# The experts' first product as seven quarter products, with operands streamed from DRAM

## The chip, the cores and the metric

One Trainium2 chip, and on it one core. The metric is the device time of one execution in microseconds (us). A core has TensorE (PE in the profile, with its weight loads as PEld), VectorE (DVE), ScalarE (ACT), GpSimd (POOL) and SyncE (SP), each with its own queue of instructions; the DMAs of this kernel are issued from SP.

## What is computed

Three stages follow one another: attention with feature maps, a first MLP, and a layer of 8 experts, all of which see all 2304 tokens. The experts' weights are 8 x 512 x 1024 and 8 x 1024 x 512:

```
x = attention(q, k, v, w_phi)                 # 4 batches, 8 heads, 576 tokens -> 2304 x 512
h = x @ w_in                                  # float64 weights, 512 x 2048
x = (h * clip(h + 3, 0, 6) / 6) @ w_out       # 2304 x 512
P = exp(x @ w_gate - max)                     # 2304 x 8, then 8 rounds of:
    P /= P.sum(1) ; P /= P.sum(0) ; P *= N / E
for e in range(8):
    out += P[:, e:e+1] * (maximum(x @ w1[e], 0) @ w2[e])
```

## The kernel before, in words

A float32 product is made of three matmuls on halves of the operands: a value is rounded to its high part (ScalarE's `hi_act` or GpSimd's `hi_pool`), the low part is the difference (`lo_dve` or `lo_pool`), and `mm3` (L79 to L82) adds high x high, high x low and low x high in one PSUM bank. All matmuls pass through L80, L81 and L82, so the profile has to be read by the names of the banks and operands. The eight banks are four named acc, two att, one h and one kv; the sums of the experts' first product go to h and kv in turn, those of the second product to acc.

The tokens are held in SBUF with features on partitions as `x_hi` and `x_lo` (128 x 4 x 2304 each, L99 and L100), and five `chunks` cut them: four of 512 tokens and one of 256.

**First phase.** Attention goes through 16 pairs of heads; the first MLP (`mlp`, L368) through four groups of tokens, the first three with a chunk each, the last (group 3) with 512 and 256 tokens. A group has 16 steps `f` of 128 hidden features. The weights of a step come by SP as `wf`, and GpSimd splits them into `wh` and `wl` (L137 to L152; two or three buffers each). While groups 0 to 2 run, attention's pairs are interleaved with their steps (L552 to L564); beside group 3 stand the gates (`gate`, L452) of three chunks and the load of the first expert weights. At the end of a group its sums, in the four acc banks (and the two att banks for the 256 tokens), are written to `x_hi` by ScalarE and to `x_lo` by VectorE (L420 to L425).

**Second phase.** The 32 `units` are an expert and a quarter of its 1024 features, 256 each. For each unit SP loads 512 KB of `w1` and of `w2` one unit ahead, and GpSimd splits them into `wah`, `wal`, `wbh`, `wbl` (`expert_weights`, L428). For each chunk the first product makes two tiles of 128 features, 12 matmuls each (4 parts of the inner dimension x 3), as wide as the chunk; ScalarE makes the high half `hh` of the relu (L665), VectorE the low half `hl` (L666). The second product (`second`, L625) is made for the chunk before: for each 128 tokens 6 matmuls of 512 columns into an acc bank, which VectorE adds, times the gate's weight, to `acc` in SBUF (L642). The rounds on P (`sinkhorn`, L580) are advanced by one step after each tile of features in the first units. The order on each engine follows the order in which the code is written; buffers and banks are handed on by semaphores.

## Time and profile before

| what | value |
|---|---|
| median of 3 runs | 2335.61 us (2333.55 to 2335.96) |
| profiled execution, its span | 2340.8 us |
| PE busy | 2292.3 us, 98%, 10855 matmuls |
| VectorE, ScalarE, GpSimd busy | 1135.3, 545.1, 657.8 us |
| attention, first MLP | up to 719 us |
| experts | 719 to 2336 us |
| DMA traffic | 104.58 MB, mean 45 GB/s |

The profiled execution has no time of its own beside its span, which is 5.2 us above the median of the runs. PE is busy almost from end to end; most of the traffic falls in the first 560 us, and in the experts the DMAs have little to do. Matmuls are pipelined, so the busy time of one (395 ns for 512 columns) is longer than the distance to the next; what counts is the distance between starts.

### The profile page before, as it was taken

To read this page: it belongs to the slowest core of one execution; us is meant where nothing else is said; L and a number is where in the kernel's file an instruction comes from. 1 tells how busy PE (TensorE), PEld (TensorE's weight loads), DVE (VectorE), ACT (ScalarE), POOL (GpSimd) and SP (SyncE) were. 2 spreads that over 40 slices of the span, in tenths; PEclk is the share of its full clock that TensorE was granted. 3 is DMA by queue.
4 is the path that set the end of the run, shared out by engine and by line. 5 is a ranking of instruction groups with operands and counts; after the bars stand their busy time and mean duration, and the time that the engine had idled before them with its cause. 6 is when DMAs were issued, how large, how long until landed. Compare 5 with 4: busy or idle time off the path is not lost.

```text
span 2340.8 us, 26890 instructions
## 1 busy us (share of the span) xinstructions
PE 2292.3 (98%) x10855; PEld 1870.0 (80%) x10855; DVE 1135.3 (49%) x1591; ACT 545.1 (23%) x1071; POOL 657.8 (28%) x553
## 2 busy tenths in 40 slices
PE   8888999999999999999999999999999999999999
PEld 6676788787888788888888888888888888888887
DVE  6899876766233433344343344343334343334343
ACT  5566554544223111111111111111111111111110
POOL 2555777777440221111111111111111111111110
PEclk9999999999999999999999999999999999999999
DMA  4355322213210000000000000000000001000002
GB/s 119 101 160 156 111 80 75 80 60 108 76 51 1 19 19 28 27 18 18 19 19 27 27 19 18 18 19 28 28 18 18 19 18 27 27 19 18 10 1 81
DMA packets 106763, 104.58 MB, mean 45 GB/s; under 512 B 61200, under 2 KB 85904, under 8 KB 106640
## 3 DMA queue, kind: packets, MB, share of 16 engines
q1 hardware_dynamic: 106640, 102.86, 14.6%
q8 instruction: 86, 1.41, 0.2%
q14 instruction: 37, 0.30, 0.0%
HBM read 89.74 MB, written 13.11 MB: 44 GB/s over the span
## 4 chain that ended last, share of the span: by engine, by line
PE 85%; DVE 9%; ACT 2%; issue 2%; POOL 2%; DMA 0%; SPq 0%; POOLq 0%; DVEq 0%; ACTq 0%
PE ps_acc L81 13%; PE ps_acc L80 13%; PE ps_acc L82 13%; PE ps_h L80 7%; PE ps_h L81 7%; PE ps_h L82 7%; PE ps_kv L80 6%; PE ps_kv L81 6%; PE ps_kv L82 6%; DVE dn L352 2%; PE ps_att L80 1%; PE ps_att L82 1%; PE ps_att L81 1%; DVE xn L354 1%; DVE gl L411 1%
## 5 line engine op out<-in xcount | busy, mean ns | idle before, releaser
L642 DVE SCALAR_TENSOR_TENSOR acc<-ps_acc,pm,acc 128x512 f32<-128x512 f32 x540 | 405.6, 751 | 271.9 <-PE ps_acc L82 263.2
L81 PE MATMUL ps_acc<-wbl,hh 128*128 128x512 f32 x1152 | 455.6, 395 | 0.0
L80 PE MATMUL ps_acc<-wbh,hh 128*128 128x512 f32 x1152 | 455.1, 395 | 0.0
L82 PE MATMUL ps_acc<-wbh,hl 128*128 128x512 f32 x1152 | 452.4, 393 | 0.0
L665 ACT ACTIVATE hh<-ps_kv 128x512 fp32r<-128x512 f32 (+1 forms) x160 | 88.8, 555 | 1079.8 <-PE ps_kv L82 1079.8
L70 POOL TENSOR_SCALAR wah<-raw 128x1024 fp32r<-128x1024 f32 x32 | 34.3, 1072 | 980.5 <-PE ps_h L81 980.5
L666 DVE SCALAR_TENSOR_TENSOR hl<-ps_kv,hh 128x512 fp32r<-128x512 f32 (+1 forms) x160 | 102.1, 638 | 364.9 <-ACT hh L665 364.9
L82 PEld LDWEIGHTS ps_acc<-wbh,hl 128*128 128x128 f32 x1152 | 217.1, 188 | 49.9
L80 PEld LDWEIGHTS ps_acc<-wbh,hh 128*128 128x128 f32 x1152 | 217.2, 189 | 49.4
L81 PEld LDWEIGHTS ps_acc<-wbl,hh 128*128 128x128 f32 x1152 | 217.3, 189 | 46.0
L666 DVE SCALAR_TENSOR_TENSOR hl<-ps_h,hh 128x512 fp32r<-128x512 f32 (+1 forms) x160 | 102.1, 638 | 288.2 <-ACT hh L665 288.2
L80 PE MATMUL ps_h<-x_hi,wah 128*128 128x512 f32 (+1 forms) x640 | 238.6, 373 | 0.0
L81 PE MATMUL ps_kv<-x_lo,wah 128*128 128x512 f32 (+1 forms) x640 | 238.4, 373 | 0.0
L82 PE MATMUL ps_h<-x_hi,wal 128*128 128x512 f32 (+1 forms) x640 | 238.3, 372 | 0.0
L82 PE MATMUL ps_kv<-x_hi,wal 128*128 128x512 f32 (+1 forms) x640 | 238.2, 372 | 0.0
L81 PE MATMUL ps_h<-x_lo,wah 128*128 128x512 f32 (+1 forms) x640 | 238.2, 372 | 0.0
L80 PE MATMUL ps_kv<-x_hi,wah 128*128 128x512 f32 (+1 forms) x640 | 238.1, 372 | 0.0
L76 POOL TENSOR_TENSOR wl<-wf,wh 128x512 fp32r<-128x512 f32 x128 | 173.0, 1351 | 11.1 <-PE ps_h L82 0.9
L665 ACT ACTIVATE hh<-ps_h 128x512 fp32r<-128x512 f32 (+1 forms) x160 | 88.9, 556 | 316.1 <-PE ps_h L82 316.1
L80 PEld LDWEIGHTS ps_kv<-x_hi,wah 128*128 128x128 f32 x640 | 120.2, 188 | 24.6
L82 PEld LDWEIGHTS ps_h<-x_hi,wal 128*128 128x128 f32 x640 | 120.6, 188 | 23.4
L81 PEld LDWEIGHTS ps_kv<-x_lo,wah 128*128 128x128 f32 x640 | 120.1, 188 | 24.0
(237 smaller groups left out, 3555.1 us busy)
## 6 DMA issues: line engine op xcount, KB each, us to landing
raw<-in_moe_w_dram SPq DMA_DIRECT2D x64, 512.0 KB, 3.6
wf<-scratch SPq DMA_DIRECT2D x48, 512.0 KB, 3.2
raw<-in_moe_w_in_dram SPq DMA_DIRECT2D x16, 512.0 KB, 3.7
raw<-in_moe_w_out_dram SPq DMA_DIRECT2D x16, 512.0 KB, 3.7
scratch<-wf SPq DMA_DIRECT2D x16, 512.0 KB, 3.3
kr<-in_k_dram SPq DMA_DIRECT2D x32, 128.0 KB, 2.8
...
```

Source lines behind the costliest of these rows:

```text
L70: nc.gpsimd.tensor_scalar(dst, src, 1.0, 1.0, op0=ALU.mult, op1=ALU.mult)
L76: nc.gpsimd.tensor_tensor(out=dst, in0=src, in1=f32(hi), op=ALU.subtract)
L80: nc.tensor.matmul(o, lhsT=wh, rhs=xh, start=start, stop=False, skip_group_check=chk)
L81: nc.tensor.matmul(o, lhsT=wh, rhs=xl, start=False, stop=False, skip_group_check=chk)
L82: nc.tensor.matmul(o, lhsT=wl, rhs=xh, start=False, stop=stop, skip_group_check=chk)
L352: nc.vector.reciprocal(out=dn[:, cs], in_=dn[:, cs])
L354: nc.vector.tensor_tensor(out=xn[:, cs], in0=xn[:, cs], in1=dn[:, cs], op=ALU.mult)
L411: nc.vector.scalar_tensor_tensor(out=gl, in0=ug, scalar=1.0 / 6.0, in1=f32(gh), op0=ALU.mult, op1=ALU.subtract)
L642: nc.vector.scalar_tensor_tensor(out=a, in0=ps, scalar=pm[:, ti, e:e + 1], in1=a, op0=ALU.mult, op1=ALU.add)
L665: nc.scalar.activation(hh[:, 0:n], ps, AF.Relu)
L666: nc.vector.scalar_tensor_tensor(out=hl[:, 0:n], in0=ps, scalar=0.0, in1=f32(hh[:, 0:n]), op0=ALU.max, op1=ALU.subtract)
```

## The change

The tokens are no longer held as `x_hi` and `x_lo` over the whole kernel. For a full chunk (512 tokens) x is cut in four quarters, by the halves of the inner dimension (b1., b2.) and the two halves of the tokens; the weights of an expert likewise in four (a11 to a22), by halves of the features and of the inner dimension. Seven products of sums of quarters, after Strassen and in Winograd's form, take the place of eight: `t1 x s1`, `b11 x a11`, `b22 x s4`, `t2 x s2`, `b21 x a12`, `t3 x s3`, `t4 x a22`. Each is 12 matmuls of 256 columns.

- At the end of a group of the MLP `quarters` copies the sums out (ScalarE), makes four differences (GpSimd), and `x_out` splits each of the seven operands (ScalarE, VectorE) in one of two buffers `xo` and stores it to DRAM, 512 KB each, by SP. The last chunk, of 256 tokens, leaves as `k1` and `k2` and is multiplied in the old way, in matmuls of 256 columns.
- In the experts the operands are read back, in the order of their use, into a ring of five tiles `xr`, four ahead, anew for each of 16 `blocks`. A block is an expert and half of its features (two times 256), so 30 operands of 512 KB a block. Eight weight tiles of 256 KB come with it; GpSimd makes four sums and splits eight operands `w1o` and four `w2o`.
- The products are added up partly in PSUM: t1 and b22 in one att bank, b11, t2, t3 and t4 in one bank h or kv, b21 in another att bank; ScalarE copies three intermediate states out to tiles `u`, VectorE adds banks to them three times, and the relu's halves of three of the four quarters are made from SBUF.
- The second product adds 12 matmuls instead of 6 in a bank, and VectorE adds to `acc` half as often. `PATTERN` says in which order products (U) and output tiles of the chunk before (D) come: UUDUUUUDU for the first chunk of a block, UUDUUDUUDUD for the others, UDDUDD for the last.
- The gates' products are made in the first block, from the operands in the ring, and the rounds on P advance by one step with each output tile.
- In the MLP `x` lies in tiles by chunk, and attention's writes to it are cut at the borders of chunks. The weights of block 0 are loaded and prepared in group 3.

The core of the diff:

```diff
-    x_hi = const.tile([P, KD, NT], F32R, name="x_hi")
-    x_lo = const.tile([P, KD, NT], F32R, name="x_lo")
...
+    XOPS = ("b11", "b21", "b22", "t4", "t1", "t2", "t3")
+    xs = [
+        {o: dram.tile([P, 4 * HF], F32, name="xs_%d_%s" % (ci, o)) for o in (XOPS if n == CH else ("k1", "k2"))}
+        for ci, (_, n) in enumerate(chunks)
+    ]
...
         for ci in parts:
-            c0, n = chunks[ci]
-            for dd in range(KD):
-                o, _ = rows(ci, dd)
-                hi_act(x_hi[:, dd, c0:c0 + n], o)
-                lo_dve(x_lo[:, dd, c0:c0 + n], o, x_hi[:, dd, c0:c0 + n])
-        yield
...
+            if chunks[ci][1] == CH:
+                quarters(ci, [rows(ci, dd)[0] for dd in range(KD)])
+            else:
+                for i, o in enumerate(("k1", "k2")):
+                    x_out(ci, o, acc[ci, i].rearrange("p (k t) -> p k t", k=2))
+        yield
+    def x_out(ci, name, src):
+        t = xe.tile([P, 2, 2, HF], F32R, tag="xo", name="xo", bufs=2)
+        hi_act(t[:, 0], src)
+        lo_dve(t[:, 1], src, t[:, 0])
+        nc.sync.dma_start(xs[ci][name], f32(t).rearrange("p h k t -> p (h k t)"))
...
+        def sub(a, b, tag):
+            t = cv.tile([P, 2, HF], F32, tag=tag, name="xt")
+            nc.gpsimd.tensor_tensor(out=t, in0=a, in1=b, op=ALU.subtract)
+            return t
+        t1 = sub(b12, b11, "t")
+        t2 = sub(b22, t1, "u")
+        for name, src in (("t1", t1), ("b11", b11), ("b22", b22), ("t2", t2), ("b21", b21)):
+            x_out(ci, name, src)
+        x_out(ci, "t3", sub(b22, b12, "t"))
+        x_out(ci, "t4", sub(b21, t2, "u"))
...
-    def expert_weights(e, j):
-        tiles = []
-        for src, nm, kk, n in (
-            (w1[e, :, j * FB:(j + 1) * FB].rearrange("(k p) f -> p k f", p=P), "wa", KD, FB),
-            (w2[e, j * FB:(j + 1) * FB, :].rearrange("(k p) d -> p k d", p=P), "wb", FT, DM),
-        ):
-            raw = wp.tile([P, kk, n], F32, tag="raw2", name="raw2", bufs=3)
-            nc.sync.dma_start(raw, src)
-            th = wp.tile([P, kk, n], F32R, tag=nm + "h", name=nm + "h")
-            tl = wp.tile([P, kk, n], F32R, tag=nm + "l", name=nm + "l")
-            hi_pool(th, raw)
-            lo_pool(tl, raw, th)
-            tiles += [th, tl]
-        return tiles
...
+    FH, QB = FE // 2, 2
+    BF = QB * P
+    NJ = FH // BF
+    blocks = [(e, j) for e in range(E) for j in range(NJ)]
+    wops, w2t, raw = {}, {}, {}
+    def w_load(b):
+        e, j = blocks[b]
+        for r in range(2):
+            for k in range(2):
+                t = wp.tile([P, 2, BF], F32, tag="raw2", name="raw2", bufs=8)
+                src = w1[e, k * HF:(k + 1) * HF, r * FH + j * BF:r * FH + (j + 1) * BF]
+                nc.sync.dma_start(t, src.rearrange("(k p) f -> p k f", p=P))
+                raw[b, "a%d%d" % (r + 1, k + 1)] = t
...
+    def halves(tag, bufs, src):
+        t = (wp if tag == "w1o" else hp_).tile([P, 2] + list(src.shape[1:]), F32R, tag=tag, name=tag, bufs=bufs)
+        hi_pool(t[:, 0], src)
+        lo_pool(t[:, 1], src, t[:, 0])
+        return t
...
+        def keep(o, src):
+            wops[b, o] = halves("w1o", 12, src)
+        s1 = add(a["a21"], a["a22"], ALU.add)
+        keep("s1", s1)
+        s2 = add(s1, a["a11"], ALU.subtract)
+        yield
+        keep("s4", add(a["a12"], s2, ALU.subtract))
+        yield
+        keep("s2", s2)
+        yield
+        keep("s3", add(a["a11"], a["a21"], ALU.subtract))
+        yield
+        for o in ("a11", "a12", "a22", "a21"):
+            keep(o, a[o])
+            yield
...
+    ORDER = ("t1", "b11", "b22", "t2", "b21", "t3", "t4")
+    WITH = {"t1": "s1", "b11": "a11", "b22": "s4", "t2": "s2", "b21": "a12", "t3": "s3", "t4": "a22"}
+    units = [(b, c) for b in range(len(blocks)) for c in range(len(chunks))]
+    wanted = [(c, o) for _, c in units for o in (ORDER if chunks[c][1] == CH else ("k1", "k2"))]
+    XR = 5
+    xring = []
+    def x_ahead(n):
+        while len(xring) < min(n, len(wanted)):
+            c, o = wanted[len(xring)]
+            t = wp.tile([P, 2, 2, HF], F32R, tag="xr", name="xr", bufs=XR)
+            nc.sync.dma_start(f32(t).rearrange("p h k t -> p (h k t)"), xs[c][o])
+            xring.append(t)
...
-            elif im % 6 == 0:
-                next(gates, 0)
-                if im == 48:
-                    prefetch(0)
+            elif im == 8:
+                w_load(0)
+                first = w1_prep(0)
+            elif im % 8 == 0:
+                take(first, 1)
+            elif im == 120:
+                x_ahead(XR - 1)
...
+    def product(ps, w, x, fresh):
+        for q in range(QB):
+            qs = slice(q * P, (q + 1) * P)
+            o = ps[:, q * HF:(q + 1) * HF]
+            for k in range(2):
+                mm3(o, w[:, 0, k, qs], w[:, 1, k, qs], x[:, 0, k, :], x[:, 1, k, :], fresh and q == 0 and k == 0, True, True)
+    def relu_halves(src):
+        t = hp_.tile([P, 2, CH], F32R, tag="h", name="h", bufs=HB)
+        nc.scalar.activation(t[:, 0], src, AF.Relu)
+        nc.vector.scalar_tensor_tensor(out=t[:, 1], in0=src, scalar=0.0, in1=f32(t[:, 0]), op0=ALU.max, op1=ALU.subtract)
+        return t
...
+        def step(o, ps, fresh):
+            i = n0 + ORDER.index(o)
+            x_ahead(i + XR)
+            product(ps, wops[b, WITH[o]], xring[i], fresh)
+            if b == 0 and o in ("t1", "b11", "b22", "b21"):
+                if o == "t1":
+                    gate_ps.append(bank("acc"))
+                kh, tokens = {"t1": (0, [1]), "b11": (0, [0, 1]), "b22": (1, [1]), "b21": (1, [0])}[o]
+                gate_add(xring[i], kh, tokens, o == "t1")
...
+        def plus(t, ps):
+            nc.vector.tensor_tensor(out=t, in0=ps, in1=t, op=ALU.add)
+            return t
...
+        xp = bank("att")
+        step("t1", xp, True)
+        p5 = kept(xp)
+        yield
+        ap = a_bank()
+        step("b11", ap, True)
+        p1 = kept(ap)
+        yield
+        step("b22", xp, False)
+        p53 = kept(xp)
+        yield
+        step("t2", ap, False)
+        c12 = plus(p53, ap)
+        got["12"] = relu_halves(c12)
+        yield
+        xp = bank("att")
+        step("b21", xp, True)
+        c11 = plus(p1, xp)
+        yield
+        step("t3", ap, False)
+        c22 = plus(p5, ap)
+        got["22"] = relu_halves(c22)
+        got["11"] = relu_halves(c11)
+        yield
+        step("t4", ap, False)
+        got["21"] = relu_halves(ap)
...
+        e, j = blocks[b]
+        ps = bank("acc")
+        ts_ = slice(t * P, (t + 1) * P)
+        for i in range(2 * QB):
+            h = (h1, h2)[i // QB].rearrange("p h (q t) -> p h q t", q=QB)[:, :, i % QB, ts_]
+            w = w2t[b, i]
+            mm3(ps, h[:, 0], h[:, 1], w[:, 0], w[:, 1], i == 0, i == 2 * QB - 1)
...
+    PATTERN = {(7, 0): "UUUUUUU", (7, 4): "UUDUUDUUDUD", (7, 2): "UUDUUUUDU", (2, 4): "UDDUDD"}
...
+        for s in PATTERN[steps, len(behind)]:
+            if s == "U":
+                next(u)
             else:
+                outputs(*behind.pop(0))
...
+        if coming is not None:
+            take(coming, {0: 1, 1: 2, 2: 1, 3: 5, 4: 0}[c])
+            take(late, {1: 1, 2: 1}.get(c, 0))
```

PE in the middle of the expert loop, before: one chunk of a unit, from the first product in bank kv on (`wah`, `wal` are the halves of w1, `wbh` those of w2); between the rows shown stand the other passes of the same operands.

```order
L80 MATMUL ps_kv_11523<-x_hi_74,wah_11137 128x512
L81 MATMUL ps_kv_11523<-x_lo_75,wah_11137 128x512
L82 MATMUL ps_kv_11523<-x_hi_74,wal_11138 128x512
...
L80 MATMUL ps_h_11540<-x_hi_74,wah_11137 128x512
...
L80 MATMUL ps_acc_11557<-wbh_11143,hh_11486 128x512
...
L80 MATMUL ps_acc_11557<-wbh_11143,hh_11503 128x512
```

PE at a like place of the changed kernel, the first matmul of each product of one chunk (t1, b11, then an output tile, b22, t2) and of the four weights of the output tile.

```order
L80 MATMUL ps_att_12010<-xr_11895,w1o_11145 128x256
...
L80 MATMUL ps_h_12027<-xr_11914,w1o_11703 128x256
...
L80 MATMUL ps_acc_12044<-w2o_11336,h_11910 128x512
...
L80 MATMUL ps_acc_12044<-w2o_11522,h_11910 128x512
...
L80 MATMUL ps_acc_12044<-w2o_11981,h_11944 128x512
...
L80 MATMUL ps_att_12010<-xr_11929,w1o_11330 128x256
...
L80 MATMUL ps_h_12027<-xr_11964,w1o_11333 128x256
```

Each product takes a new tile of the ring, and a product is half as wide; the output tile has four weights in place of two.

GpSimd at the start of group 3, before: between the weights of the group's first steps (`wh`, `wl`) it splits the weights of the first two units of the experts (`wah` to `wbl`).

```order
L70 TENSOR_SCALAR wah_6328<-raw2_6326 128x1024
L76 TENSOR_TENSOR wal_6329<-raw2_6326,wah_6328 128x1024
L70 TENSOR_SCALAR wh_5843<-wf_5837 128x512
L70 TENSOR_SCALAR wbh_6334<-raw2_6332 128x1024
L76 TENSOR_TENSOR wl_5844<-wf_5837,wh_5843 128x512
L76 TENSOR_TENSOR wbl_6335<-raw2_6332,wbh_6334 128x1024
...
L70 TENSOR_SCALAR wbh_7096<-raw2_7094 128x1024
L76 TENSOR_TENSOR wl_5840<-wf_5837,wh_5839 128x512
L76 TENSOR_TENSOR wbl_7097<-raw2_7094,wbh_7096 128x1024
L70 TENSOR_SCALAR wh_5938<-wf_5936 128x512
```

GpSimd at the start of group 3 in the changed kernel: `xt` are differences of quarters of x, `ws` sums of weights, `w1o` their halves; `wh_6029` and `wh_6025` belong to the second step of the group, `wh_6123` to the third.

```order
L476 TENSOR_TENSOR xt_5926<-xf_5920 128x512
L596 TENSOR_TENSOR ws_6173<-raw2_6079,raw2_6081 128x512
L70 TENSOR_SCALAR wh_6029<-wf_6023 128x512
L70 TENSOR_SCALAR w1o_6175<-ws_6173 128x512
L476 TENSOR_TENSOR xt_5928<-xf_5923,xt_5926 128x512
...
L70 TENSOR_SCALAR wh_6025<-wf_6023 128x512
L70 TENSOR_SCALAR w1o_6258<-ws_6256 128x512
...
L76 TENSOR_TENSOR w1o_6655<-raw2_6081,w1o_6655 128x512
L70 TENSOR_SCALAR w1o_6734<-raw2_6079 128x512
L76 TENSOR_TENSOR w1o_6734<-raw2_6079,w1o_6734 128x512
L70 TENSOR_SCALAR wh_6123<-wf_6121 128x512
```

All of block 0's sums and splits, and the differences of chunk 2, now stand in one row ahead of the third step's weights; before it is four operands of twice the size, each split in two halves.

PE at the hand-over from the MLP to the experts, before: the last matmuls of the MLP in an att bank, and the first of the experts.

```order
L80 MATMUL ps_att_5923<-gh_7008,wh_6900 128x256
L81 MATMUL ps_att_5923<-gl_7009,wh_6900 128x256
L82 MATMUL ps_att_5923<-gh_7008,wl_6901 128x256
L80 MATMUL ps_kv_7100<-x_hi_74,wah_6328 128x512
L81 MATMUL ps_kv_7100<-x_lo_75,wah_6328 128x512
```

PE at the hand-over in the changed kernel: the MLP's last sums are in the att banks 6107 and 6114, the experts' first product t1 wants such a bank (7307), b11 does not.

```order
L80 MATMUL ps_att_6114<-gh_7179,wh_7071 128x256
L81 MATMUL ps_att_6114<-gl_7180,wh_7071 128x256
L82 MATMUL ps_att_6114<-gh_7179,wl_7072 128x256
L726 MATMUL ps_acc_7330<-xr_7308,wg_74 16x256 x4
L80 MATMUL ps_kv_7337<-xr_7310,w1o_6497 128x256
...
L726 MATMUL ps_acc_7330<-xr_7316,wg_74 16x256 x4
L80 MATMUL ps_att_7307<-xr_7308,w1o_6175 128x256
```

Behind b11 and the gate's matmuls everything on PE stands behind the product that needs an att bank.

## Rows read from the trace of the kernel before

**Rows 1.** The page, busy time by engine, and the chain that ended last.

```profile
PE 2292.3 (98%) x10855; PEld 1870.0 (80%) x10855; DVE 1135.3 (49%) x1591; ACT 545.1 (23%) x1071; POOL 657.8 (28%) x553
...
PE 85%; DVE 9%; ACT 2%; issue 2%; POOL 2%; DMA 0%; SPq 0%; POOLq 0%; DVEq 0%; ACTq 0%
```

**Rows 2.** Stretches: window, length; PE, PEld, DVE, ACT, POOL busy; clock; DMA share; GB/s.

```profile
560.00:580.00 20.00, 19.82 (x94) 16.12 (x93) 11.96 (x16) 9.78 (x18) 15.21 (x14) 1.00 0.55 185
...
772.00:774.00 2.00, 2.00 (x6) 1.54 (x6) 1.76 (x8) 0.00 (x0) 0.00 (x0) 0.50 0.78 247
900.00:1200.00 300.00, 300.00 (x1366) 246.26 (x1365) 119.26 (x168) 33.33 (x60) 41.46 (x24) 1.00 0.07 22
100.00:200.00 100.00, 88.71 (x421) 68.94 (x422) 96.43 (x135) 60.38 (x122) 62.59 (x53) 0.98 0.52 160
```

**Rows 3.** PE in time (start, us, operation): group 3's start, first and last expert matmul.

```profile
573.37 0.40 PE L80 MATMUL ps_h<-x_hi,wh 128*128 128x512 f32 x1
...
719.41 0.39 PE L80 MATMUL ps_kv<-x_hi,wah 128*128 128x512 f32 x1
...
2335.78 0.39 PE L82 MATMUL ps_acc<-wbh,hl 128*128 128x512 f32 x1
```

**Rows 4.** PE's waits, from 300 to 575 us and from 575 us on.

```profile
PE ps_att L214 <- ACT xn L348: 4.4, 5, 0.9
...
PE ps_att L603 <- DVE c L601: 2.5, 1, 2.5
PE ps_kv L80 <- ACT lt L462: 1.0, 1, 1.0
PE ps_kv L466 <- DVE u L407: 0.8, 1, 0.8
```

**Rows 5.** PE in time, runs of 24 narrow and 24 wide matmuls, first and next.

```profile
1020.93 0.28 PE L80 MATMUL ps_kv<-x_hi,wah 128*128 128x256 f32 x1
...
1023.76 0.40 PE L80 MATMUL ps_acc<-wbh,hh 128*128 128x512 f32 x1
...
1029.27 0.40 PE L80 MATMUL ps_kv<-x_hi,wah 128*128 128x512 f32 x1
...
1034.87 0.40 PE L80 MATMUL ps_acc<-wbh,hh 128*128 128x512 f32 x1
```

**Rows 6.** VectorE's addition to acc: ns, minimum, median, maximum.

```profile
L642 DVE SCALAR_TENSOR_TENSOR acc<-ps_acc,pm,acc x540: 749/751/754, 844.3 to 2336.2; 128x512 f32<-128x512 f32 x180
```

**Rows 7.** DMA issues (size, us to landing), and one issue on SP.

```profile
raw<-in_moe_w_dram SPq DMA_DIRECT2D x64, 512.0 KB, 3.6
...
scratch<-wf SPq DMA_DIRECT2D x16, 512.0 KB, 3.3
...
276.17 0.54 SPq L144 DMA_DIRECT2D wf<-scratch  x1
```

**Rows 8.** GpSimd in time (start, us): the two halves of a split.

```profile
561.32 0.62 POOL L70 TENSOR_SCALAR wh<-wf 128x512 fp32r<-128x512 f32 x1 [1.57 <-PE ps_h L81]
...
565.60 1.30 POOL L76 TENSOR_TENSOR wl<-wf,wh 128x512 fp32r<-128x512 f32 x1
```

**Rows 9.** PE in time around its one long pause in the experts.

```profile
771.52 0.39 PE L603 MATMUL ps_att<-c,ones 128*128 128x8 f32 x2 [2.48 <-DVE c L601]
771.77 0.65 PE L81 MATMUL ps_acc<-wbl,hh 128*128 128x512 f32 x1
...
775.19 0.46 PE L80 MATMUL ps_acc<-wbh,hh 128*128 128x512 f32 x1
```

**Rows 10.** The halves of x from banks: durations, minimum, median, maximum.

```profile
L67 ACT ACTIVATE x_hi<-ps_acc x16: 572/598/604, 276.5 to 718.2; 128x512 fp32r<-128x512 f32 x16
...
L73 DVE TENSOR_TENSOR x_lo<-ps_acc,x_hi x16: 670/692/692, 277.1 to 718.8; 128x512 fp32r<-128x512 f32 x16
```

**Rows 11.** VectorE's operation on pm, all eight, and GpSimd beside the longest.

```profile
L600 DVE TENSOR_TENSOR pm<-pm,r x8: 307/309/2071, 748.8 to 791.8; 128x144 f32<-128x144 f32 x8
...
768.51 2.35 POOL L76 TENSOR_TENSOR wal<-raw,wah 128x1024 fp32r<-128x1024 f32 x1
```

More of the change, by code (lines that the diff above doesn't have):

```diff
@@ L508, in tile_kernel @@
                 load_consts()
-    actx = mctx.enter_context(ExitStack())
     at = actx.enter_context(tc.tile_pool(name="at", bufs=1, reuse_waits="tile"))
@@ new lines, in halves, with w1_prep, add @@
+    def halves(tag, bufs, src):
[3 more added lines that the diff above has]
+        return t
+    def w1_prep(b):
+        a = {o: raw.pop((b, o)) for o in ("a11", "a12", "a21", "a22")}
+        def add(x, y, op):
+            t = wp.tile([P, 2, BF], F32, tag="ws", name="ws", bufs=3)
+            nc.gpsimd.tensor_tensor(out=t, in0=x, in1=y, op=op)
+            return t
[14 more added lines that the diff above has]
+            yield
@@ L674, in tile_kernel, with gate_add, gate_end @@
-    second(*pend)
+    gate_ps = []
+    def gate_add(x, kh, tokens, first=False):
+        for k in range(2):
+            for h in range(2):
+                for t in tokens:
+                    nc.tensor.matmul(
+                        gate_ps[-1][0:2 * E, t * HF:(t + 1) * HF], lhsT=wg[:, 2 * kh + k, :], rhs=x[:, h, k, :],
+                        start=first and k == 0 and h == 0 and t == tokens[0], stop=True, skip_group_check=True,
+                    )
+    def gate_end(c):
+        c0, n = chunks[c]
+        lt = hp_.tile([2 * E, CH], F32, tag="u", name="lt", bufs=UB)
+        nc.scalar.copy(lt[:, 0:n], gate_ps.pop(0)[0:2 * E, 0:n])
+        yield
+        ps = bank("acc")
+        for i in range(n // P):
+            nc.tensor.matmul(ps[:, i * E:(i + 1) * E], lhsT=lt[:, i * P:(i + 1) * P], rhs=sel, start=True, stop=True)
+        nc.vector.tensor_copy(
+            lg[:, c0 // P:(c0 + n) // P, :], ps[:, 0:(n // P) * E].rearrange("p (t e) -> p t e", e=E)
+        )
+        yield
@@ L678 @@
+    for x in behind:
+        outputs(*x)
 _INS = ['q', 'k', 'v', 'w_phi', 'moe_w_in', 'moe_w_out', 'moe2_w_gate', 'moe2_w1', 'moe2_w2']
```

223 lines of the change are left out of this document (136 added, 87 removed).

## The prediction

> **What bounds the kernel now.** I read the page first: PE is busy 98% of the span, VectorE 49%, GpSimd 28%, ScalarE 23%, and 85% of the chain that ended last is PE, 13% of it in each of the three lines that write ps_acc [rows 1]. Then the table of stretches: from 900 to 1200 us PE is busy in all 300 us at the full clock, with 1366 matmuls, while the DMAs carry 22 GB/s [rows 2]. A unit of the expert loop has 4 x 48 + 36 = 228 matmuls, so it takes 228 x 300 / 1366 = 50.07 us, and the 32 units 1602 us: the whole time from the first expert matmul at 719.41 to the last at 2335.78 but for some 14 us [rows 3]. Behind the last matmul stands one addition and a store. The list of waits shows that PE waits three times from 575 us on, 4.3 us in all, but for a rest of 0.2 [rows 4]. So in the experts PE's matmuls set the time, one for one, and whatever takes matmuls away there is gained as long as nothing else begins to hold PE.
>
> The profiled span is 2340.8 us, the median of the runs 2335.61, 5.2 us less. All sums below are differences within the profiled execution; I subtract them from the median.
>
> **First product, the gain.** What a matmul costs is the distance of the starts, not the busy time of one. A run of 24 matmuls of 512 columns goes from 1029.27 to 1034.87, 0.2333 us each; 24 of 256 columns from 1020.93 to 1023.76, 0.1179 us each [rows 5]. Halving the columns thus costs about 1% extra. For one chunk of 512 tokens and 512 features before has 48 x 0.2333 = 11.20 us; seven products of 12 narrow matmuls are 84 x 0.1179 = 9.90. That is 1.295 us saved, in 16 blocks x 4 chunks = 64 places: **-82.9 us**. The last chunk keeps 48 narrow matmuls, as two units have together. The new matmuls alternate between banks (att and h or kv), which before also does without a gap; I charge nothing.
>
> The Trainium skill (TensorE: Matmul & The Clock Gate, "Back-to-back issue gap") puts the distance at columns / 2.4 ns plus about 2.5 ns, 215.8 and 109.2 ns; by it the saving would be 64 x (48 x 0.2158 - 84 x 0.1092) = 76 us. The trace has 233.3 and 117.9 ns here, and I keep the rows.
>
> **Second product.** 18 token tiles x 64 feature tiles x 3 matmuls of 512 columns, before and after: 0. VectorE loses about half of 540 additions of 751 ns [rows 6], off PE's path, since PE never waited for one. The sums stay twice as long in a bank, and four banks are there.
>
> **Gates.** They leave the MLP and the small idle gaps there; block 0 gets 88 matmuls of 256 columns, 10.4 us, where before has 32 x 0.2333 + 8 x 0.1179 = 8.4: **+2.0**.
>
> **Steady state.** Each block reads 30 operands of 512 KB and 2 MB of weights, 17.8 MB, in 2 x 50.07 - 4 x 1.295 = 95.0 us: 188 GB/s, where before has 22. Nearest rows: from 560 to 580 us the queues carried 185 GB/s at a DMA share of 0.55, and in 2 us 247 at 0.78 [rows 2], so there is room. Latency: a 512 KB transfer lands 3.3 to 3.6 us after its issue, and an issue holds the queue 0.54 us [rows 7]. The ring has five tiles and runs four ahead. Its tightest place is the first chunk of a block, where four quarter products follow with no output tile between: a tile comes free 4 x 12 x 0.1179 = 5.65 us before its need, against 0.6 + 3.6 = 4.2. The other tight place is the second chunk, where three weight loads stand ahead of operands on SP until GpSimd has split the weights before them; by the order and the durations above I get an arrival about 2.5 us ahead of need. GpSimd has 12 splits and 4 additions a block: 12 x (0.62 + 1.30) + 4 x 1.30 (an addition taken as the low half, the other operation on two operands of that size) = 28.2 us of 95 [rows 8]. VectorE has three sums with a bank, 0.69, and four low halves a chunk, some 5 us, and four additions of output tiles, 3 us, of 21. So I count 0 for the steady state; a gain is excluded, since PE had no idle time to give, and on the dear side the bounds are the rivals below.
>
> **Start of the last MLP group (near 573 us).** Here GpSimd's queue gets 4 subtractions, 4 additions and 8 splits between the weights of the second and the third step of features: 8 x 1.30 + 8 x 1.92 = 26 us [rows 8]. Before splits four operands of twice the size there, some 4 x 2 x 1.92 = 15 us, without a pause for wh [rows 4]. A step takes (719.41 - 573.37) / 16 = 9.1 us [rows 3], and PE has the weights of two, 18 us of work, after some 5 us of pauses, as the first weights too wait behind subtractions that wait for ScalarE's copies. The third step's weights are split about 30 us after the start and wanted after 23. Placing GpSimd's instructions in their order I get pauses of about 2 and 3 us at the start and 7 at the third step, and none behind: a step needs 2 x 1.92 us of GpSimd in 9.1, so it catches up. Before waits 1.8 us at the same place for lt and u [rows 4]. After a pause the clock is lost too: 2.48 us of idle time at 769 us is followed by matmuls 0.4275 us apart, a clock of 0.50, until 775.2, 8 matmuls x 0.2 = 1.6 us [rows 9, 2]. Sum 12 + 1.6 - 1.8 = **+11.5**, bounds 0 (splits run beside ScalarE earlier than I place them) and 20.
>
> **Hand-over to the experts (near 719 us).** Nine operands must leave: each a high half on ScalarE, 0.60, a low half on VectorE, 0.69 [rows 10], and a store of 512 KB, 3.3 [rows 7], before one of two buffers is free: two leave every 4.6 us. The last two, k1 and k2, come from the att banks. PE meanwhile does one product and gate matmuls, 3.8 us, and then wants an att bank, which comes free when k1's low half is done: four copies of whole banks, 4 x 0.6, and three turns of the two buffers, 3 x 4.6, 16.3 us after the hand-over. That is 12.5 us of idle time; the other att bank and its operand (a load that stands on SP behind the stores) add little over 1. Idle about 13.8 us, and a clock loss of 1.6: **+15.4**, bounds 5 and 25. Before has no such pause there [rows 3].
>
> **The rest.** Spreading the normalisation removes the one stall of 2.48 us and its clock loss: **-4**. At the ends of groups 0 to 2 copies, subtractions and stores come between attention's work; PE waits there now for xn on ScalarE [rows 4]: **+5**, bounds 0 and 15. Attention's x at borders of chunks is written in two pieces: +1.
>
> Sum: -82.9 + 2.0 + 11.5 + 15.4 - 4 + 5 + 1 = -52; 2335.6 - 52 = **2284 us**.
>
> **Rivals.**
> (A) The pauses are dearer, or operands are late here and there. With all bounds at their high ends the sum is -82.9 + 2 + 20 + 25 - 4 + 15 + 1 = -24, 2312 us; 0.2 us per chunk more in the loop makes 2325. For it: each of the three places is a new chain over three engines and a queue, and I placed it by hand.
> (B) The other side: **the stream of operands paces the blocks**. For it: nothing in before streams for long; the highest mean of 100 us is 160 GB/s [rows 2], and a block would then take 17.8 MB / 160 = 111 us, 16 us more than PE's 95, +262 in all: 2284 + 262 = 2546. Against it: that stretch was not held by DMA (share 0.52). It decides from 52 / 16 = 3.3 us of waiting a block, that is at 181 GB/s sustained, or where transfers land 5 us after their issue in place of 3.6.
> (C) **GpSimd holds VectorE.** One VectorE multiplication of two operands in SBUF took 2.07 us, with a GpSimd subtraction of 2.35 us begun about it, where its median is 0.31; the additions that read a bank never exceed 754 ns over 540 [rows 11, 6]. After, three low halves a chunk read SBUF twice; where GpSimd holds them, the banks that they and the sums ahead need are late. At 1 us a chunk 64 us come back: 2284 + 64 = 2348. Against it: GpSimd is busy under a third of a block, and PE needs a half only some products later.
> The Trainium skill (SBUF — State Buffer, "Who interferes with whom") states that a VectorE instruction with two inputs in SBUF and a GpSimd one that reads SBUF exclude each other for a whole instruction, and that one with a single input there is free. The 2.07 us and the 754 ns agree.
> (D) The pauses are smaller, as the splits and stores overlap better: all low bounds, -82.9 + 2 + 5 - 4 + 1 = -79, 2257 us.
>
> **How the numbers follow.** Forecast (2270 to 2300) 0.55, A 0.18, B 0.10, C 0.06, D 0.11. The range runs from D's 2255 to A's 2325; it leaves out B, C and some 0.02 of the others, 0.18. Faster by over 0.2%, about what a measurement of this kernel can tell from no change (4.7 us, so below 2331), is the forecast, D and most of A: 0.82; within it, the rest of A: 0.04; slower: B and most of C: 0.14.
>
> **What would show it.** In the changed kernel's stretches of the expert loop PE should stay 99% busy at clock 1.00 with DMA near 188 GB/s and share 0.56; the narrow matmuls should start 0.118 us apart; a block should take 95 us. The waits should name the operands (xr) hardly at all, GpSimd's wh near 590 to 610 us, and the att bank's release on VectorE after the hand-over. It is wrong if PE waits for xr every block, if the narrow matmuls are further apart beside the stream, or if the hand-over costs more than 25 us.

## The result, and the profile after

The changed kernel takes 2311.28 us (median of 4 runs, 2309.93 to 2311.96), the kernel before 2335.78 beside it: a ratio of 0.9889, interval 0.9871 to 0.9908. It is faster by 24.5 us, where 52 were forecast. The time lies inside the stated range, outside the forecast's own 2270 to 2300, and at the number of case A, "the pauses are dearer"; it does not come about by A's sum, as the account below shows.

The page's first part, after; beside [rows 1], GpSimd has gone from 658 to 936 us and ScalarE from 545 to 668, PE from 2292 to 2227:

```profile
PE 2227.2 (97%) x13207; PEld 1952.3 (85%) x13207; DVE 1105.8 (48%) x1486; ACT 668.3 (29%) x1270; POOL 936.0 (41%) x895
```

Stretches of the changed kernel (columns as in [rows 2]): the start of the last MLP group, the hand-over, and 300 us in the middle of the experts:

```profile
575.00:620.00 45.00, 33.80 (x146) 27.68 (x145) 23.40 (x24) 15.58 (x30) 38.99 (x37) 0.81 0.54 195
...
720.00:760.00 40.00, 28.82 (x173) 25.59 (x172) 11.72 (x17) 12.68 (x23) 12.49 (x13) 0.86 0.30 118
...
1200.00:1500.00 300.00, 300.00 (x1891) 272.45 (x1890) 117.26 (x153) 55.68 (x95) 89.70 (x86) 1.00 0.56 186
```

The loop is as forecast: PE busy in all 300 us at clock 1.00, DMA share 0.56, 186 GB/s. The losses stand where PE is not busy: 11 us of 45 at the start of the group, 11 of 40 at the hand-over. PE's three largest waits over the whole span name the hand-over (VectorE's xo), attention (ScalarE's xn, spread over seven places) and the MLP's u:

```profile
PE ps_att L80 <- DVE xo L73: 11.2, 1, 11.2
PE ps_att L240 <- ACT xn L374: 8.6, 7, 2.2
PE ps_h L80 <- DVE u L438: 8.2, 3, 7.0
```

One block, from an output tile's first matmul to the same of the next block, and a run of 24 narrow matmuls within one (PE in time):

```profile
1457.81 0.40 PE L80 MATMUL ps_acc<-w2o,h 128*128 128x512 f32 x1
...
1553.17 0.40 PE L80 MATMUL ps_acc<-w2o,h 128*128 128x512 f32 x1
...
1401.66 0.28 PE L80 MATMUL ps_att<-xr,w1o 128*128 128x256 f32 x1
...
1404.53 0.40 PE L80 MATMUL ps_acc<-w2o,h 128*128 128x512 f32 x1
```

A block takes 95.36 us (forecast 95.0), and a narrow matmul (256 columns) 2.87 / 24 = 0.1196, where [rows 5] had 0.1179.

**How the first phase is read.** Both kernels have 64 steps in the MLP. The time by which a step's first matmul stands behind the same one of the kernel before is a running account of what the change has cost so far. The end of group 0, before and after:

```profile
279.88 0.48 PE L80 MATMUL ps_h<-x_hi,wh 128*128 128x512 f32 x1
...
287.47 0.39 PE L80 MATMUL ps_h<-x_hi,wh 128*128 128x512 f32 x1
```

```profile
280.12 0.48 PE L80 MATMUL ps_h<-xhi,wh 128*128 128x512 f32 x1
...
295.96 0.63 PE L80 MATMUL ps_h<-xhi,wh 128*128 128x512 f32 x1
```

The lag goes from 0.24 to 8.49 us in one step. Worked out in this way for the kernels that follow (us behind the kernel before, at the start of the step; from step 4 of group 2 to the start of group 3 no lag moves by more than 0.6):

| kernel | group 1, step 0 | step 1 | group 2, step 0 | step 4 | group 3, step 1 | step 2 | step 15 |
|---|---|---|---|---|---|---|---|
| changed | 0.2 | 8.5 | 8.3 | 15.4 | 22.1 | 26.3 | 21.8 |
| e1, four buffers xo | -1.0 | 6.4 | 7.3 | 16.5 | 22.2 | 19.7 | 22.2 |
| e2, three buffers wf | -0.3 | 8.7 | 9.0 | 16.9 | 24.0 | 28.2 | 24.3 |
| e6, eight products | 1.2 | 4.0 | 3.0 | 3.2 | 3.1 | -0.9 | -8.4 |
| e7, block 0 held back | -0.5 | 8.5 | 8.9 | 14.4 | 22.3 | 20.8 | 14.5 |
| e8, no low halves | -0.8 | 5.8 | 5.5 | 9.0 | 12.5 | 10.7 | 15.8 |
| e11, no differences | 1.0 | 2.8 | 3.1 | 7.7 | 7.7 | 5.7 | 8.4 |
| e10, e7 with e1 | -0.1 | 7.3 | 8.2 | 17.3 | 23.3 | 20.7 | 13.1 |
| e12, e10 with differences on VectorE | 0.9 | 5.5 | 6.6 | 11.0 | 15.2 | 12.5 | 5.0 |

In the first column the end of group 0 has only begun, and the rows already differ by up to 1.2 us: differences of that size are not read. Group 3 has lost the gates' matmuls and waits. What that gives back is seen in e6, where little else is late: 11.4 us, from 3.1 to -8.4. That the other kernels get as much back is an estimate; in most of them other losses within the group use it up.

### The profile page after: what moved, and what is told of

Read it like the earlier page. It is cut to its first block, busy times and chain, and to the rows that moved or that the text cites. A ratio compares the mean times of both kernels' runs of the same rounds, so it can differ in the third digit from the quotient of the medians.

```text
span 2307.9 us, 33330 instructions
## 1 busy us (share of the span) xinstructions
PE 2227.2 (97%) x13207; PEld 1952.3 (85%) x13207; DVE 1105.8 (48%) x1486; ACT 668.3 (29%) x1270; POOL 936.0 (41%) x895
## 4 chain that ended last, share of the span: by engine, by line
PE 66%; DVE 1%; DMA 1%; ACT 0%; issue 0%; ACTq 0%
PE ps_acc L80 11%; PE ps_acc L81 11%; PE ps_acc L82 11%; PE ps_att L80 4%; PE ps_att L82 4%; PE ps_att L81 4%; PE ps_kv L80 3%; PE ps_kv L82 3%; PE ps_kv L81 3%; PE ps_h L80 3%; PE ps_h L82 3%; PE ps_h L81 3%; PE ps_acc L726 0%; DMA xs_b<-xo 0%; DMA xr<-xs_t 0%; PE ps_acc L738 0%
## 5 line engine op out<-in xcount | busy, mean ns | idle before, releaser
L80 PE MATMUL ps_acc<-w2o,h 128*128 128x512 f32 x1152 | 451.8, 392 | 0.0
L81 PE MATMUL ps_acc<-w2o,h 128*128 128x512 f32 x1152 | 451.6, 392 | 0.0
L82 PE MATMUL ps_acc<-w2o,h 128*128 128x512 f32 x1152 | 448.5, 389 | 0.0
L856 DVE SCALAR_TENSOR_TENSOR acc<-ps_acc,pm,acc 128x512 f32<-128x512 f32 x252 | 188.7, 749 | 432.5 <-PE ps_acc L82 431.3
L82 PEld LDWEIGHTS ps_acc<-w2o,h 128*128 128x128 f32 x1152 | 216.6, 188 | 46.9
L80 PEld LDWEIGHTS ps_acc<-w2o,h 128*128 128x128 f32 x1152 | 217.3, 189 | 38.2
L81 PEld LDWEIGHTS ps_acc<-w2o,h 128*128 128x128 f32 x1152 | 217.4, 189 | 35.5
L80 PE MATMUL ps_att<-xr,w1o 128*128 128x256 f32 x768 | 219.1, 285 | 13.1 <-DVE xo L73 11.2
L762 ACT ACTIVATE h<-u 128x512 fp32r<-128x512 f32 x192 | 114.3, 627 | 373.0 <-DVE u L789 373.0
L763 DVE SCALAR_TENSOR_TENSOR h<-u,h 128x512 fp32r<-128x512 f32 x192 | 177.2, 950 | 89.9 <-ACT h L762 89.9
L82 PE MATMUL ps_att<-xr,w1o 128*128 128x256 f32 x768 | 218.7, 285 | 0.0
L81 PE MATMUL ps_att<-xr,w1o 128*128 128x256 f32 x768 | 218.6, 285 | 0.0
L785 ACT COPY u<-ps_att 128x512 f32<-128x512 f32 x128 | 75.1, 587 | 428.8 <-PE ps_att L82 428.8
L80 PE MATMUL ps_kv<-xr,w1o 128*128 128x256 f32 x640 | 181.4, 283 | 0.0
L82 PE MATMUL ps_kv<-xr,w1o 128*128 128x256 f32 x640 | 181.3, 283 | 0.0
L80 PE MATMUL ps_h<-xr,w1o 128*128 128x256 f32 x640 | 181.3, 283 | 0.0
L82 PE MATMUL ps_h<-xr,w1o 128*128 128x256 f32 x640 | 181.3, 283 | 0.0
L81 PE MATMUL ps_h<-xr,w1o 128*128 128x256 f32 x640 | 181.3, 283 | 0.0
L81 PE MATMUL ps_kv<-xr,w1o 128*128 128x256 f32 x640 | 181.3, 283 | 0.0
L76 POOL TENSOR_TENSOR wl<-wf,wh 128x512 fp32r<-128x512 f32 x128 | 174.2, 1361 | 10.2
L80 PEld LDWEIGHTS ps_att<-xr,w1o 128*128 128x128 f32 x768 | 148.1, 193 | 19.5 <-DVE xo L73 11.5
```

What stands on the lines that cost most here:

```text
L76: nc.gpsimd.tensor_tensor(out=dst, in0=src, in1=f32(hi), op=ALU.subtract)
L80: nc.tensor.matmul(o, lhsT=wh, rhs=xh, start=start, stop=False, skip_group_check=chk)
L81: nc.tensor.matmul(o, lhsT=wh, rhs=xl, start=False, stop=False, skip_group_check=chk)
L82: nc.tensor.matmul(o, lhsT=wl, rhs=xh, start=False, stop=stop, skip_group_check=chk)
L762: nc.scalar.activation(t[:, 0], src, AF.Relu)
L763: nc.vector.scalar_tensor_tensor(out=t[:, 1], in0=src, scalar=0.0, in1=f32(t[:, 0]), op0=ALU.max, op1=ALU.subtract)
```

## The experiments

The kernel before, measured beside these runs, had medians from 2334.2 to 2340.4 us. So a few us between the times of two experiments show little by themselves, and the lags and waits of the traces carry the argument.

**The buffers and the order of the stores (e1 to e4).** Theory R: ScalarE waits for one of two buffers. Theory W: the stores are late because SP stands before a weight load. Theory P: it is the added work on GpSimd, ScalarE and VectorE itself. For R and W speaks the start of group 3 after (SP, then ScalarE): the weight load goes out at 605.71, the store behind it at 606.12, and ScalarE had idled 10.14 us for such a store:

```profile
605.71 0.32 SPq L168 DMA_DIRECT2D wf<-scratch  x1
606.12 0.39 SPq L463 DMA_DIRECT2D xs_b<-xo  x1
...
611.17 0.63 ACT L67 ACTIVATE xo<-xf 128x512 fp32r<-128x512 f32 x1 [10.14 <-DMA xs_b<-xo]
```

```diff
-        t = xe.tile([P, 2, 2, HF], F32R, tag="xo", name="xo", bufs=2)
+        t = xe.tile([P, 2, 2, HF], F32R, tag="xo", name="xo", bufs=4)
```

> Edit: four buffers xo in place of two. In the changed kernel the first phase runs 8.4 us behind the kernel before after the end of group 0, 7.0 more after group 1, 10.9 more at the start of group 3 (6.4 after the gates are gone), and PE idles 11.2 us on VectorE's xo at the hand-over. Theory R (ScalarE waits for an xo buffer, that is for the store of the piece two before, and everything behind it on ScalarE and VectorE waits too): the hand-over's wait falls to about 5 us, the three lags to about 5, 4 and 6; in all -16, 2295 us. Theory W (the stores are late because SP stands before a weight load wf that waits for GpSimd): most of the lags falls too, since four pieces go ahead without a store, same 2295. Theory P (the additional work on GpSimd, ScalarE and VectorE itself): lags as they are, only the hand-over's wait falls by some 6: 2305.

Measured 2304.42 us, ratio 0.9851 (0.9824 to 0.9879). The hand-over's wait fell from 11.2 to 6.1, as expected. The lags did not come down. At step 2 of group 3 the lag is 6.6 us less, but the gain is lost by step 7 (21.5 beside 21.9), and what PE waits for there now are GpSimd's halves of the MLP's weights (e1, PE's waits from 575 to 760 us):

```profile
PE ps_att L80 <- DVE xo L73: 6.1, 1, 6.1
PE ps_h L80 <- DVE u L438: 6.0, 1, 6.0
PE ps_h L80 <- POOL wh L70: 4.2, 2, 3.6
PE ps_h L82 <- POOL wl L76: 2.8, 4, 1.1
```

So the buffers set the hand-over, and not the first phase.

```diff
-        wf = cv.tile([P, 2, DM], F32, tag="wf", name="wf")
+        wf = cv.tile([P, 2, DM], F32, tag="wf", name="wf", bufs=3)
```

> Edit: three buffers wf for the MLP's weights in place of two; xo stays at two. Theory W: SP issues the next wf without waiting for GpSimd, the stores behind it leave at once, and the lags of 8.4, 7.0 and 10.9 us fall to about 5, 4 and 5; the hand-over, where no wf is loaded, keeps its 11.2 us: -12, 2299 us. Theory R with the stores' own 3.3 us as the pace: lags change by under 1 us each: 2310. Theory P: no change, 2311.

Measured 2310.59 us (0.9879, 0.9851 to 0.9907); no lag fell. W is out: the wait on SP was there, and cost nothing that something else did not cost as well.

```diff
-        for ci in parts:
+        for ci in reversed(parts):
```

> Edit: at the end of group 3 the two pieces of the last chunk (k1, k2, from the att banks) are split and stored first, the seven of chunk 3 after them. Theory of the prediction (PE's idle time at the hand-over is the wait for an att bank at the end of the row of nine pieces): the wait of 11.2 us for xo is gone at its place; but ScalarE's copy of the first product (u) now stands behind the seven other pieces, so PE gains only what it can do meanwhile, two products and gate matmuls, 3 to 5 us: 2307. Rival (the att bank is not the point, the operands' loads behind the stores on SP are): no change, 2311. The ends of groups 0 to 2 stay as they are.

Measured 2314.0 us (0.9891, 0.9861 to 0.992). The wait for xo is gone at its place, and 8.4 us for an operand's load, which SP now issues behind more stores, have come instead. The att bank is the wait that ended last, as predicted, but its removal alone gains nothing.

> Edit: the three edits together. If R and W are both in it, the lags of the first phase come down to about 12 us in all from 22, and the hand-over costs 5 us in place of 18 (idle time and clock): 2311 - 10 - 13 = 2288 us. If P holds: lags stay at 22, hand-over 5: 2298.

Measured 2307.18 us (0.986, 0.9826 to 0.9893): no better than e1 alone. The hand-over waits 4.9 us for an operand and 3.0 for ScalarE's u.

**The kernel before, again (e5).**

> Edit: none, the kernel before again, for a second trace. Its profiled execution was 5.2 us above the median of its runs, and the sum of the prediction was made inside it. If that surplus lies in the first phase (attention, up to 719 us), the new trace starts the experts near 714 us and needs the same 1621 us from there; if it lies in the experts, 719 and 1616.

Measured 2334.01 us. The second trace starts the experts at 719.67 and spans 2333.9. In 300 us of the loop it has 1372 matmuls where [rows 2] has 1366:

```profile
900.00:1200.00 300.00, 300.00 (x1372) 246.86 (x1371) 119.39 (x168) 33.39 (x60) 41.41 (x24) 1.00 0.07 22
```

A unit takes 49.92 us in place of 50.15, 32 x 0.23 = 7.4 us: the surplus lay in the experts, at the same granted clock. It did not lie in the matmuls that the change takes away. The runs of [rows 5] in this trace, 24 narrow, 24 wide of the second product, 24 wide of the first:

```profile
1020.16 0.28 PE L80 MATMUL ps_kv<-x_hi,wah 128*128 128x256 f32 x1
...
1022.91 0.39 PE L80 MATMUL ps_acc<-wbh,hh 128*128 128x512 f32 x1
...
1028.40 0.39 PE L80 MATMUL ps_kv<-x_hi,wah 128*128 128x512 f32 x1
...
1034.00 0.39 PE L80 MATMUL ps_acc<-wbh,hh 128*128 128x512 f32 x1
```

The wide matmuls of the first product take 5.60 us in both traces. The narrow ones are 0.1144 us apart in place of 0.1178; those of the second product, over twelve pairs of units, 0.2294 in place of 0.2308.

**The products (e6).** Core of the edit:

```diff
-    XOPS = ("b11", "b21", "b22", "t4", "t1", "t2", "t3")
+    XOPS = ("b11", "b21", "b12", "b22")
...
-    PATTERN = {(7, 0): "UUUUUUU", (7, 4): "UUDUUDUUDUD", (7, 2): "UUDUUUUDU", (2, 4): "UDDUDD"}
+    PATTERN = {(4, 0): "UUUU", (4, 4): "UDUDUDUD", (4, 2): "UDUUDU", (2, 4): "UDDUDD"}
```

> Edit: eight products in place of seven (four quarters of x stored and streamed, 96 matmuls of 256 columns a full chunk, no sums of weights or of x, no sums of products); the stream, the blocks and the doubled sums of the second product stay. If the seven products give what the count says, 12 matmuls x 0.1195 us x 64 chunks = 92 us come back, a block takes 95.36 + 4 x 12 x 0.1195 = 101.1 us, less some 10 us for three operands fewer at each end of a group: 2395 us, 2.5% slower than the kernel before. Rival (the stream or the sums of products cost PE something in the seven that the trace does not show): the block takes under 100 us.

Measured 2358.26 us, ratio 1.0094 (1.0074 to 1.0113). A block takes 101.12 us:

```profile
1457.67 0.40 PE L80 MATMUL ps_acc<-w2o,h 128*128 128x512 f32 x1
...
1558.79 0.40 PE L80 MATMUL ps_acc<-w2o,h 128*128 128x512 f32 x1
```

That is 5.76 more than with seven, 92.2 in 16 blocks, to the microsecond what the count of 12 x 0.12 x 64 gives. But the kernel is only 47 us slower than the changed one by the medians, and 50.3 by the two traces: in these its first phase is 30.2 us shorter (table, -8.4 against 21.8) and the hand-over with the first blocks 11.7. Seven products gain 92 us here; to make their operands, the sums of weights included, costs 42 to 45 of them. And 16 x (101.12 - 2 x 49.92) = 20.5 us are what the same eight products cost more in narrow matmuls than in wide ones.

**What the first phase waits for (e7, e8, e11).**

```diff
+                held = [wp.tile([P, 2, 2, BF], F32R, tag="w1o", name="w1o", bufs=12) for _ in range(12)]
...
+                    nc.vector.tensor_tensor(out=jk, in0=f32(held.pop(0)[:, 0, 0, 0:1]), in1=f32(LT[0][:, 0:1]), op=ALU.add)
```

> Edit: block 0's halves of weights are held back, one operand w1o for each step of the last MLP group (a tiny VectorE instruction on a late tile frees each buffer), so that GpSimd does not make them all in a row at the start of group 3. GpSimd theory (four differences, four additions and eight splits in a row delay the MLP's weights and, through them, all else): the lag of the first phase, 15.4 us at the start of group 3 and 21.8 at its end in the changed kernel, grows by 2 us or less within group 3: 2306 us or less. Rival (the seven pieces with their two buffers hold ScalarE and VectorE): PE still waits some 7 us for u at the second step, lag 20 to 22: 2310.

Measured 2303.65 us (0.9865, 0.9844 to 0.9886). The lag is 14.4 at the start of group 3 and 14.5 at its end, 7.3 us less than in the changed kernel, as the theory of GpSimd has it. But the wait for u at the second step has stayed (8.1 us), as the rival has it: both are in it, one behind the other.

```diff
-        lo_dve(t[:, 1], src, t[:, 0])
-        nc.sync.dma_start(xs[ci][name], f32(t).rearrange("p h k t -> p (h k t)"))
+        for h in range(2):
+            nc.sync.dma_start(xs[ci][name][:, h * 2 * HF:(h + 1) * 2 * HF], f32(t[:, 0]).rearrange("p k t -> p (k t)"))
```

> Edit: the low halves of the operands stored are left out (VectorE does nothing for a piece; the high half is stored in both places by two stores of half the size), so the low passes of the experts multiply other numbers; PE's work is unchanged. If VectorE's seven subtractions, stretched from 0.69 to 1.1 to 1.8 us beside GpSimd, make the ends of groups 0 and 1 long, the lags of 8.4 and 7.0 us fall to about 4 each, the hand-over's wait falls by 3: 2298 us. If ScalarE's copies or the wait for buffers make them, the lags change by 1 us or less: 2309.

One run, 2302.8 us: the steps of 8.3 and 7.1 us at the ends of groups 0 and 1 become 6.6 and 3.5; the wait at the hand-over is 10.2 us, where a fall by 3 was expected. VectorE's halves are a part of it, about half at the second end and less at the first.

```diff
-            nc.gpsimd.tensor_tensor(out=t, in0=a, in1=b, op=ALU.subtract)
-            return t
+            return a
```

> Edit: GpSimd's four differences at the end of a group are left out (quarters stand in for the sums, so the products are of other numbers); seven pieces are still split and stored. With four pieces and no differences the eight-product kernel lagged only 2.8 and 0 us at the ends of groups 0 and 1, with seven and the differences 8.2 and 7.0. If the differences (four GpSimd operations of 1.3 to 1.7 us, beside which VectorE's halves are stretched) make that, the lags fall to about 4 and 2, and in group 3 by 5: 2300 us. If the three more pieces make it, they stay within 2 us: 2310.

One run, 2295.96 us: the steps become 1.8 and 4.6 us, and that at the start of group 3 is gone (7.7 us at both of its first steps). So it is above all the differences, not the number of pieces. (The edit also frees the buffers that the differences share with the MLP's t and u. e12 below keeps them shared, and its steps fall by less: the buffers may have a part in what e11 gains beyond it.) The differences also hold VectorE. Its low halves of quarters in SBUF (xf), nanoseconds minimum, median and maximum, in the changed kernel, and in e11 (all seven of a group):

```profile
L73 DVE TENSOR_TENSOR xo<-xf,xo x12: 693/1147/1764, 283.8 to 750.0; 128x512 fp32r<-128x512 f32 x12
```

```profile
L73 DVE TENSOR_TENSOR xo<-xf,xo x28: 669/727/2170, 279.1 to 740.1; 128x512 fp32r<-128x512 f32 x28
```

The median falls from 1147 to 727 ns when GpSimd's differences are gone; the same subtraction from a bank takes 692 [rows 10]. The two rows are not quite alike, since 16 of the 28 pieces were differences before, with a median of 692 then already; e12 has the same twelve. Counted in the traces over all 28 pieces, the halves above 0.8 us are 17 in the changed kernel, 13 in e11 and 7 in e12, and each of them runs beside a GpSimd instruction. This is the prediction's rival C, at another place.

**The margin of the stream (e9).**

```diff
-    XR = 5
+    XR = 3
```

> Edit: a ring of three operand tiles in place of five. It measures how near the stream is to pacing the blocks (the prediction's rival B). In the changed kernel a block takes 95.36 us and PE never waits for xr from the second block on; a transfer lands 4.1 us after its issue. With five tiles the shortest time from release to need is four products, 5.7 us; with three it is two products, 2.9 us, where products follow without an output tile, against 0.4 + 4.1 = 4.5. If that arithmetic holds, PE waits some 1.6 us at five or six places of each block: +8 to +10 us a block, 2311 + 140 = 2450 us. Rival (the loads are issued far enough ahead anyway, as two tiles come free almost together): under 2 us a block, below 2345.

Measured 2363.58 us, ratio 1.0111 (1.0091 to 1.0132). PE waits for operands some 30 times from 900 us on, 1 us each on the mean, and most blocks take 97 to 100 us:

```profile
PE ps_att L80 <- DMA xr<-xs_b: 10.5, 10, 2.0
PE ps_h L80 <- DMA xr<-xs_b: 9.6, 11, 1.6
PE ps_h L80 <- DMA xr<-xs_t: 8.0, 9, 1.5
```

Neither the 140 us nor the "under 2 us a block" came: waits of up to 2.0 us where 1.6 were reckoned, but at a third of the places. (Of the 52 us, 7.4 stand in the first phase already; why, no run shows.) With five tiles there is no such wait behind the hand-over, though a transfer under this load takes longer than [rows 7] (to landing, minimum, median, maximum, in the changed kernel):

```profile
DMA to landing us min/median/max: 3.1/4.1/7.5
```

**Together (e10, e12).** e10 is e7 with e1's four buffers.

> Edit: the held-back preparation of block 0 and four buffers xo together. Each alone gave 7 us at another place (start of group 3; hand-over). If the two causes are apart, the gains add up: lag 14.5 us through group 3 and 5 us less at the hand-over, 2311 - 7.5 - 6 = 2298 us. If both only move a wait that GpSimd or VectorE sets anyway, 2303 to 2305.

Measured 2294.9 us, ratio 0.9817 (0.9796 to 0.9837), 16.4 below the changed kernel, where the two edits alone gave 6.9 and 7.6: the two causes are apart, and add up. The traces say the same: the hand-over's wait is 6.1 us, as in e1, and the lag at the end of group 3 is 13.1, beside 14.5 in e7. e12 moves the differences to VectorE, one operand of each from a bank:

```diff
-            nc.gpsimd.tensor_tensor(out=t, in0=a, in1=b, op=ALU.subtract)
+            for k in range(2):
+                nc.vector.tensor_tensor(out=t[:, k], in0=a[k], in1=b[k], op=ALU.subtract)
...
-        t1 = sub(b12, b11, "t")
+        t1 = sub(p12, (b11[:, 0], b11[:, 1]), "t")
```

> Edit: held-back preparation and four buffers xo as in the run before, and the four differences of a group's end moved from GpSimd to VectorE, which reads the sums straight from the banks (eight operations of 256 columns, some 0.42 us each by the halves of that size, 3.4 us a group). Without the differences at all the lags at the ends of groups 0 and 1 were 2.1 and 4.6 us, with them on GpSimd some 8 and 9. If it is GpSimd's queue, and its hold on VectorE's halves beside it, that costs: the lags fall to about 5 and 4, and the time by some 7, 2294.9 - 7 = 2288 us. If VectorE is the engine that PE waits for there in any case, 3.4 us more for it eat what is gained: 2295 us or above.

Measured **2285.4 us**, ratio 0.9785 (0.9769 to 0.9801): 50.6 us below the kernel before, 25.9 below the changed one, better than both. The steps at the ends of groups 0 and 1 are 4.6 and 4.4 us (7.4 and 9.1 in e10), that at the start of group 3 is 3.6 (from 11.6 at its step 0), and the halves of quarters are back at a median of 692 ns, from 1292 in e10:

```profile
L73 DVE TENSOR_TENSOR xo<-xf,xo x12: 674/692/1757, 282.8 to 729.3; 128x512 fp32r<-128x512 f32 x12
```

VectorE has 32 instructions more and is busy no longer than in e10 (1113.3 and 1114.0 us), and PE waits less.

## Why the prediction was right, and by how much it was off

Measured against e5's trace of the kernel before (span 2333.9; the changed kernel 2307.9, so -26.0):

| term | forecast | measured | where it is read |
|---|---|---|---|
| products, 16 blocks | -82.9 | -71.7 | 16 x (95.36 - 2 x 49.92) |
| ends of groups 0 and 1, split x | +6 | +15.2 | lag 0.2 to 15.4 |
| hand-over | +15.4 | +15.7 | idle 11.2, operand 1.9, clock 2.6 |
| start of group 3, gates, normalisation | +9.5 | +14.9 | lag 15.4 to 21.8; 8.5 in the rest of the experts, by subtraction |
| sum | -52 | -25.9 | |

The mechanism was right in each term, and three sizes were off: the saving is 11 us smaller than forecast, the ends of the groups cost 9 us more, and the start of group 3 with the gates 5 more. That the total comes within a microsecond of case A's 2312 is luck: A has the full saving, 25 us for the hand-over and 20 at the start of group 3, and none of the three came.

- **First product.** Right in kind, and e6 shows the count exactly; the size failed by 11 us. The mis-sized price is that of the narrow matmul, 0.1179 us. The 384 narrow matmuls of a steady block of the changed kernel start 0.1197 us apart on the mean, which takes 9.5 us from the saving; the wide ones that they replace had their price right, 0.2333 in both traces of the kernel before. The rest is the last chunk, whose narrow matmuls are dearer than in e5 (0.1144) by 4.0 us, and the second product, whose matmuls are cheaper by 2.3. The surplus of the profiled execution did not touch this term, as e5 shows. But the price did hang on the trace: by e5's narrow rows the same sum gives 64 x (48 x 0.2333 - 84 x 0.1144) = 102 us.
- **One of the prediction's signs of being wrong came, if by 1.5%:** the narrow matmuls are further apart in the changed kernel. The stream's load is not what spreads them: in the last chunk, 20 us after the last operand was sent for and at 58 GB/s in place of 186, 24 of them take 2.87 us as well:

```profile
2289.28 0.28 PE L80 MATMUL ps_h<-xr,w1o 128*128 128x256 f32 x1
...
2292.15 0.40 PE L80 MATMUL ps_acc<-w2o,h 128*128 128x512 f32 x1
...
2285.00:2300.00 15.00, 15.00 (x79) 12.91 (x78) 4.08 (x6) 0.60 (x1) 0.00 (x0) 1.00 0.22 58
```

- **Ends of groups 0 and 1.** The other mis-sized term: +5 within "0 to 15", and it was 15. It was reckoned as copies and stores between attention's work. The differences on GpSimd, with their hold on VectorE, are most of it (e11: 6.4 of 15.2 us remain without them).
- **Start of group 3.** Forecast 12 us of pauses and 1.6 of clock (with the 1.8 that go, 11.8 and not the 11.5 of the sum); the changed kernel loses some 17.8, 6.4 of lag and, as an estimate from e6, the 11.4 that the departed gates give back. GpSimd's queue is the cause, as was said (e7, 7.3 us of it; e11), but PE's waits were named wrongly: the prediction looked for wh, and the longest is u, 7.0 us. The MLP's tiles t and u share their buffers with the differences in GpSimd's queue. ScalarE's t waits 3.4 us for one of these, and VectorE's u then stands behind a stretched half:

```profile
594.58 0.69 ACT L436 ACTIVATE t<-ps_h,cst 128x512 f32<-128x512 f32 x1 [3.40 <-POOL xt L476]
...
597.47 1.75 DVE L73 TENSOR_TENSOR xo<-xt,xo 128x512 fp32r<-128x512 f32 x1
599.32 0.69 DVE L438 SCALAR_TENSOR_TENSOR u<-t,ps_h 128x512 f32<-128x512 f32 x1
```

- **Hand-over.** The best-placed term: 11.2 us of idle time before the att bank and 1.9 for the operand behind it, 13.1 where 13.8 were forecast, and by the chain that was given (e1 halves the first; PE in time and the stretch behind):

```profile
743.06 1.98 PE L726 MATMUL ps_acc<-xr,wg 128*16 128x256 f32 x16
756.23 0.58 PE L80 MATMUL ps_att<-xr,w1o 128*128 128x256 f32 x1 [11.19 <-DVE xo L73]
...
757.00:762.00 5.00, 5.00 (x25) 4.89 (x24) 0.70 (x2) 1.67 (x3) 5.00 (x6) 0.50 0.62 192
```

  The matmuls behind it ran at the lower level for 6 us, 27 of them, 2.6 us lost where 1.6 were reckoned.
- **Steady state.** 0 was right: no wait in the loop at 186 GB/s. Rival B did not come; e9 shows how near it is, two tiles of the ring away.
- **Rival C** cost PE nothing in the loop, but its mechanism is there. The low halves of the relu that read two operands in SBUF (`u`, `h`) took up to 1783 ns, while the same operation with one operand in a bank never passed 694. Of the 192 from SBUF, 57 took over 800, and each of these 57 ran beside a GpSimd instruction, where 18 of the other 135 did; of the 96 from a bank 55 did, at no cost. PE did not wait for them. Nanoseconds minimum, median and maximum, in the changed kernel:

```profile
L763 DVE SCALAR_TENSOR_TENSOR h<-u,h x192: 678/693/1783, 766.5 to 2276.2; 128x512 fp32r<-128x512 f32 x192
L763 DVE SCALAR_TENSOR_TENSOR h<-ps_kv,h x48: 677/692/694, 773.0 to 2284.7; 128x512 fp32r<-128x512 f32 x48
```

  It cost time at the ends of the groups, where GpSimd, VectorE and PE depend on one another within a few us.

What stays open: why the same program's narrow matmuls and those of its second product stand further apart in one execution than in another, why the narrow ones stand at 0.1197 in the changed kernel, and what part of the ends of groups 0 and 1 in e12 (9 us still) is ScalarE's.
